# Attention and gated MLP on one core: each batch's last four output units are made among the next batch's value units, and the planner that orders the program gets other dependencies and costs

## The chip, the core and the metric

The kernel runs on one core of one Trainium2 chip. The metric is the device time of one execution in microseconds (us). The core's engines are named as in its profile: PE (matmul; PEld is its weight load, which runs beside it), DVE, ACT and POOL (elementwise work), and SP, which here only issues DMA transfers.

## What is computed

Eight batches, eight heads each, 576 tokens, head width 64. Attention with a causal mask and a cumulative bias makes x; a gated MLP with a spatial gate follows:

```
scores = q @ k.T / 8 + min(bias, 0), causal          # bias from cumsum(max(s, 0))
x      = softmax(scores) @ v                         # heads side by side: 576 x 512 per batch
h      = gelu(x @ w_in)                              # 576 x 1024
u, v   = h[:, :512], h[:, 512:]
v_n    = layernorm(v) * g_ln
v_s    = w_sg @ v_n + b_sg[:, None]                  # mixes tokens
out    = x + (u * v_s) @ w_out
```

## The kernel before

float32 products are made as three matmuls of split operands (high and low parts), accumulated in PSUM; heads 0 to 11 use plain float32 in attention.

The MLP of a batch is cut into units. Each fills one of three PSUM banks (`psm`), taken in turn in the order in which the units are written down:

- `v0` to `v4`: value units, 128 tokens each (`v4`: 64), matmuls `psm<-wi,xs` of 512 columns. An elementwise chain follows: ACT square, DVE `vt<-vt,psm`, ACT tanh, DVE `psm<-vt,psm`, DVE statistics `bs`, `mv`, DVE `vt<-psm,mv,g_b`. The last of these is what frees the bank.
- `u00` to `u13`: twelve matmuls `psm<-xs,wi` of 288 columns (half of the tokens, 128 features), then the same gelu chain.
- `s00` to `s13`: spatial gate, matmuls `psm<-ws,vn` and `psm<-wr,vnr`; the result times u is split into `gt`.
- `o00` to `o13`: twelve matmuls `psm<-gt,wo`, one DVE operation `u<-psm,xr` (half the sum plus the residual), one store `out_t<-u`. The first digit is the token half, the second the group of 128 features.

Attention of a head has scores (`pss<-k,q`), a masked minimum on DVE (`p<-pss,mask`), exp on ACT, normalising on POOL (`p<-p,rs`), transposes on PE (`psp<-ident,r`), their evacuation to `pah`, `pal`, `pbh`, `pbl`, `pdh`, `pdl` by ACT and DVE, and the product `psx<-...,vs`, evacuated to `xr`. For heads from 8 on the raw keys and queries are loaded into one buffer (`raw<-in_kq`), split by ACT and POOL (`k<-raw`) and copied about by DMA (`q<-k`, `k<-k`).

Nothing is issued as it is written. The code records operations (class `Plan`): attention of head h at place h, and the MLP of batch b spread over places 8b + 9.6 to 8b + 17.6, its units in the order of the string `ORDER` (`ORD0` for the first batch, `ORDL` for the last). `Plan.add` notes which recorded operations touch the same part of a slot or PSUM bank. `Plan.order` then simulates the engines with the costs that `cost` gives, forward and backward for `ROUNDS` rounds, and fixes one order for each engine; the engines run these queues strictly in turn. The framework adds the real semaphores by its own rules, which are not those of `Plan.add`.

Of the kernel before, what the change touches and what calls it, by code (L numbers as in the profile page):

```python
# [17 lines left out]
B, H, S, D = 8, 8, 576, 64  # L18
# [19 lines left out]
ITW = [64, 192, 320, 448, 576]  # L38
PW = [64, 192, 384, 512, 576]

ORDER = ("v0 u00 v1 u01 v2 u02 v3 v4 u10 u11 s00 u12 u03 s01 s03 u13 s02 "
         "o00 o01 s10 o03 o02 s11 s12 s13 o11 o13 o10 o12")
ORD0 = ("v0 v1 v2 v3 v4 u00 u01 u02 u10 u11 s00 u12 u03 s01 s03 u13 s02 o00 o01 s10 o03 o02 s11 s12 s13 o11 o13 o10 o12")
ORDL = ("v0 u00 v1 v2 u01 u02 v3 v4 u10 u11 s00 u12 u03 s01 s03 u13 s10 "
        "s02 o00 o01 o03 o02 s11 s12 s13 o11 o13 o10 o12")
W5, W2 = 0.232, 0.133
WARM = 8
NQ = 8
# [4 lines left out]
           ws=(8.5, 11.0), wo=(10.5, 13.0), f0=9.6, x0=2.4)  # L53
LAT = dict(PE=304.0, ACT=136.0, DVE=136.0, POOL=185.0, SP=160.0)
PROBE = None
ROUNDS = 7
N3 = 12
XR = 14

# [5 lines left out]
def _cols(ap):  # L65
    n = 1
    for _, c in list(ap.ap)[1:]:
        n *= c
    return n


def _is_ap(x):
    return hasattr(x, "ap") and hasattr(x, "tensor")


class Plan:
# [27 lines left out]
    def add(self, eng, kind, fn, args, kw):  # L104
        if "out" in kw:
            outs, rest = [kw["out"]], list(args)
        else:
            outs, rest = [args[0]], list(args[1:])
        if kw.get("accum_out") is not None:
            outs.append(kw["accum_out"])  # L110
        ins = [x for x in rest + [v for k, v in kw.items() if k not in ("out", "accum_out")] if _is_ap(x)]
        if self.open is None or self.open.eng != eng:
            o = Op()
            o.raw = set()
            o.eng, o.calls, o.deps, o.pes, o.busy, o.done, o.dma, o.kind = eng, [], set(), [], 0.0, 0.0, 0.0, kind
            k = len(self.ops)
            self.ops.append(o)
            if self.open is not None:
                self.open = o
                self.open_k = k  # L120
        else:
            o, k = self.open, self.open_k
        o.calls.append((fn, args, kw))
        cost(o, eng, kind, outs, ins, kw)
        for aps, wr in ((ins, False), (outs, True)):
            for ap in aps:
                b = self.box(ap)
                if b is None:
                    continue
                acc = self.slots.setdefault(b[0], [])  # L130
                keep = []
                for x in acc:
                    hit = x[1] < b[2] and b[1] < x[2] and x[3] < b[4] and b[3] < x[4]
                    if hit and (wr or x[5]) and x[0] != k:
                        o.deps.add(x[0])
                        if not wr:
                            o.raw.add(x[0])
                    if not (wr and hit and x[0] != k and b[1] <= x[1] and x[2] <= b[2] and b[3] <= x[3] and x[4] <= b[4]):
                        keep.append(x)
                keep.append((k,) + b[1:] + (wr,))  # L140
                self.slots[b[0]] = keep

    def group(self):
# [2 lines left out]
    def order(self, lat=LAT, rounds=None):  # L146
# [11 lines left out]
        prio = list(range(len(ops)))  # L158
        rounds = ROUNDS if rounds is None else rounds
        for i in range(rounds):  # L160
# [122 lines left out]
def cost(o, eng, kind, outs, ins, kw):  # L283
    n = _cols(outs[0])
    if eng == "PE":
        w = _cols(kw["in_"] if kind == "transpose" else ins[0])
        if kind == "transpose":
            o.pes.append((85.0 * w / P, 58.0, 165.0))
        elif ins[0].dtype == F32R:
            o.pes.append((max(54.0, 0.836 * w), 0.4397 * n + 6.4, 165.0))  # L290
        else:
            x = 0.47 * n + 45 if w == D else 0.83 * n + 95
            o.pes.append((107.0, x, 0.0))
            o.pes.append((0.0, x, 90.0))
        return
    src = ins[0] if ins else None
    psum = any("ps" == a.tensor.name[:2] for a in outs + ins)
    b = extra = 0.0
    if eng == "SP":
        q = outs[0]  # L300
        size = n * list(q.ap)[0][1] * 4
        name = src.tensor.name
        o.dma = size / (454.0 if q.tensor.name.startswith("out") else 181.0 if name.startswith("in_") else 129.5)
        return
    if eng == "ACT":
        b = 50 + 0.84 * n + (0 if psum else 40)
        if kw.get("accum_out") is not None:
            b += 204
            extra = 92
        elif _is_ap(kw.get("scale")):  # L310
            b += 95
    elif eng == "DVE":
        if kind == "tensor_tensor_reduce":
            b = 55 + 1.07 * n + (68 if _is_ap(kw["scalar"]) else 0)
        elif kind == "bn_stats":
            b = 608
        elif kind == "memset":
            b = 0.8 * n
        elif kind in ("bn_aggr", "reciprocal"):
            b = 95  # L320
        elif outs[0].dtype == I32:
            b = 480
        else:
            b = 75 + 1.03 * n + (60 if _is_ap(kw.get("scalar")) else 0) + (0 if psum else 200)
    else:
        if kind == "tensor_tensor":
            b = 535 if kw["op"] == ALU.pow else max(160, 60 + 2.36 * n)
        elif kind in ("memset", "affine_select"):
            b = 100 + n
        elif n < 8:  # L330
            b = 175
        elif kw.get("op0") == ALU.max:
            b = 850
        else:
            b = 236 + 0.83 * n
    o.busy += b
    o.done = o.busy + {"ACT": 104, "DVE": 84, "POOL": 32}[eng] + extra

# [2 lines left out]
def tile_attn_gmlp(  # L341
# [98 lines left out]
    for kind in (F32, F32R):  # L440
        v = [pools["xr"]([P, S], kind, "e", XR - 1 - i) for i in range(3)]
# [58 lines left out]
    for c0, n in ((0, 512), (512, REM)):  # L500
        ps = ps_sc.tile([P, 512], F32, name="cps", tag="sc")
        jn = NT if c0 == 0 else 5
        for j in range(jn):
            k = P if j < NT else REM
            o = max(0, j * P - c0)
# [358 lines left out]
    def ffn(b):  # L864
# [147 lines left out]
                    pools["gt"].drop(gt[ch, c])  # L1012
            yield 0.0

        unit = {"v": v_unit, "u": u_unit, "s": s_unit, "o": o_unit}
        for w in (ORD0 if b == 0 else ORDL if b == B - 1 else ORDER).split():
            yield from unit[w[0]](int(w[1]), int(w[2:] or 0))


    steps = []  # L1020
# [2 lines left out]
    def place(t, f, *args):  # L1023
        steps.append((t, next(tick), f, args))

    def spread(gen, t0, t1, total):
        done = [0.0]

        def go():
            c = next(gen, None)  # L1030
            if c is not None:
                done[0] += c
                place(t0 + (t1 - t0) * min(1.0, done[0] / total), go)

        place(t0, go)
# [20 lines left out]
    for b in range(B):  # L1056
        t0 = 8 * b + POS["f0"]
        for c in range(NC):
            place(8 * b + max(2 * c + 2.6, POS["f0"] - POS["x0"] + 0.4 * c), xsplit, b, c)
        spread(ffn(b), t0, t0 + 8.0, 53.6)  # L1060
    while steps:
        steps.sort()
        _, _, f, args = steps.pop(0)
# [58 lines left out]
```

## Time and profile before

| | us |
|---|---|
| runs | 791.68, 792.68, 795.9 (median 792.68) |
| profiled execution, its own time | 793.47 |
| its span, first to last instruction | 791.7 |
| PE busy in the span | 757.9 |
| DVE, POOL, ACT busy | 607.6, 593.5, 572.4 |

The granted TensorE clock is 0.993 of full speed over the span. Busy times overlap between engines. From about 190 us on, one batch takes some 91 us and its pattern repeats: a stretch in which value and u units run beside attention, then one of s and o units beside attention.

### The profile page before, as it was taken

The page shows a single profiled execution, that of the slowest core. Times are in us where ns is not written, and L with a number is a line of the kernel's source. Part 1 is how long each engine was busy: PE and PEld are TensorE (multiplying, and loading weights), DVE is VectorE, ACT ScalarE, POOL GpSimd, SP SyncE. Part 2 cuts the span into 40 slices and gives each one's busy share as a digit, 9 for nine tenths or more (in the row PEclk, how much of TensorE's full clock was granted, in tenths as well). Part 3 has the DMA queues.
Part 4 walks back from the last instruction along what each step waited for, and adds up shares of the span by engine and source line. Part 5 has one row for each costly group of instructions (what it writes and reads, how often), then busy time and mean ns, then how long its engine had stood idle before and what let it go on. Part 6 is the DMA issues. An engine that isn't in the chain of part 4 may idle for free.

```text
span 791.7 us, 16704 instructions
## 1 busy us (share of the span) xinstructions
PE 757.9 (96%) x5161; PEld 678.4 (86%) x5161; DVE 607.6 (77%) x1819; ACT 572.4 (72%) x1632; POOL 593.5 (75%) x981
## 2 busy tenths in 40 slices
PE   4797999999999999999999999999999999999998
PEld 3454667999889998899989998899998998899898
DVE  6788889856996679956898579966899569975662
ACT  3798789856896578956798568966799468973341
POOL 6887888867789668886789578887688767894442
PEclk9998999999999999999999999999999999999999
DMA  8476644434343543543444353334535343410101
GB/s 259 136 209 164 169 114 109 118 96 128 97 131 83 132 119 91 133 116 104 117 112 116 99 151 101 102 97 116 148 88 133 111 105 104 125 37 32 43 7 60
DMA packets 69805, 89.30 MB, mean 113 GB/s; under 512 B 25954, under 2 KB 42212, under 8 KB 69716
## 3 DMA queue, kind: packets, MB, share of 16 engines
q1 hardware_dynamic: 69716, 88.23, 41.3%
q8 instruction: 41, 0.67, 0.4%
q14 instruction: 48, 0.39, 0.2%
HBM read 42.27 MB, written 9.73 MB: 66 GB/s over the span
## 4 chain that ended last, share of the span: by engine, by line
PE 71%; ACT 9%; DVE 9%; POOL 4%; DMA 3%; issue 3%; SPq 1%; ACTq 0%; DVEq 0%; POOLq 0%
PE psm L254 43%; PE pss L254 10%; PE psx L254 9%; PE psp L254 8%; ACT p L254 3%; DVE u L254 3%; DVE p L254 2%; DMA raw<-in_kq 1%; ACT xr L254 1%; POOL vn L254 1%; POOL p L254 1%; ACT pah L254 1%; DMA q<-in_kq 1%; ACT k L254 1%; POOL k L254 1%
## 5 line engine op out<-in xcount | busy, mean ns | idle before, releaser
L254 ACT ACTIVATE p<-p,mn 128x448 f32<-128x448 f32 (+2 forms) x300 | 167.7, 561 | 45.8 <-DVE mn L254 44.5
L254 POOL TENSOR_SCALAR p<-p,rs 128x128 f32<-128x128 f32 (+3 forms) x352 | 171.1, 495 | 26.6 <-DVE rs L254 11.4
L254 PE MATMUL pss<-k,q 128*128 128x288 f32 (+9 forms) x768 | 158.7, 322 | 13.1 <-DVE mn L254 8.2
L254 PEld LDWEIGHTS pss<-k,q 128*128 128x128 f32 (+3 forms) x768 | 119.6, 184 | 40.1 <-DVE mn L254 15.9
L254 DVE CUSTOM_DVE_ANT_0 p<-pss,mask 128x448 f32<-128x448 f32 (+2 forms) x300 | 118.4, 417 | 29.2 <-PE pss L254 28.2
L254 POOL TENSOR_TENSOR k<-raw,k 128x576 fp32r<-128x576 f32 x56 | 80.0, 1429 | 60.3 <-ACT k L254 59.4
L254 PE MATMUL psm<-gt,wo 128*128 128x288 f32 x720 | 124.2, 300 | 0.0
L254 PE MATMUL psm<-xs,wi 128*128 128x288 f32 x708 | 118.5, 304 | 0.8 <-DVE vt L254 0.6
L254 PE MATMUL psm<-ws,vn 128*128 128x288 f32 x708 | 116.3, 298 | 0.0
L254 PE MATMUL psm<-wi,xs 128*128 128x512 f32 (+1 forms) x392 | 110.7, 406 | 0.3 <-DVE vt L254 0.3
L254 PEld LDWEIGHTS psm<-gt,wo 128*128 128x128 f32 x720 | 105.4, 188 | 2.0
L254 PEld LDWEIGHTS psm<-xs,wi 128*128 128x128 f32 x708 | 99.4, 188 | 4.2 <-DVE u L254 1.5
L254 PEld LDWEIGHTS psm<-ws,vn 128*128 128x128 f32 x708 | 101.4, 188 | 0.6
L254 PE MATMUL psp<-ident,r 128*128 128x128 f32 x780 | 93.7, 241 | 7.9 <-POOL p L254 6.8
L254 PEld LDWEIGHTS psp<-ident,r 128*128 128x128 f32 x780 | 83.8, 138 | 20.1 <-POOL p L254 12.1
L254 POOL TENSOR_TENSOR gt<-u,gt 128x288 fp32r<-128x288 f32 (+1 forms) x66 | 53.0, 809 | 35.5 <-ACT gt L254 32.3
L254 PEld LDWEIGHTS psm<-wi,xs 128*128 128x128 f32 (+1 forms) x392 | 68.6, 184 | 12.7 <-DVE vt L254 0.4
L254 ACT CAST pbh<-psp 128x512 fp32r<-128x512 f32 x104 | 49.7, 478 | 25.2 <-DVE u L254 15.9
L254 DVE TENSOR_TENSOR pbl<-psp,pbh 128x512 fp32r<-128x512 f32 x104 | 57.2, 550 | 5.3 <-ACT pbh L254 4.8
L254 DVE SCALAR_TENSOR_TENSOR u<-u,psm 128x288 f32<-128x288 f32 x118 | 52.3, 444 | 9.6 <-ACT u L254 9.0
L254 ACT CAST gt<-u 128x288 fp32r<-128x288 f32 (+1 forms) x66 | 27.9, 431 | 42.3 <-DVE u L254 38.3
L254 PE MATMUL psx<-pbh,vs 128*128 128x320 f32 (+3 forms) x152 | 58.3, 414 | 0.1
(140 smaller groups left out, 1627.6 us busy)
## 6 DMA issues: line engine op xcount, KB each, us to landing
q<-k SPq DMA_DIRECT2D x168, 144.0 KB
raw<-in_kq SPq DMA_DIRECT2D x56, 288.0 KB
vr<-in_vp SPq DMA_DIRECT2D x52, 192.0 KB
out_t<-u SPq DMA_DIRECT2D x64, 144.0 KB
k<-k SPq DMA_DIRECT2D x56, 144.0 KB
gt<-in_w_in SPq DMA_DIRECT2D x16, 256.0 KB
k<-in_kq SPq DMA_DIRECT2D x8, 288.0 KB
q<-in_kq SPq DMA_DIRECT2D x8, 288.0 KB
```

Of the source, the lines that this page charges most:

```text
L254: fn(*args, **kw)
```

## The change

The string that orders the units names the four units `o11 o13 o10 o12` of the batch before (marked `-`) between `v0` and `v4`; the first batch leaves them out, the last makes its own four at its end. A batch's units are kept so that the next batch can make them. Three edits touch only the planner: two accesses to one slot now also depend on each other where the tensor names differ, or for a PSUM bank where PE writes and another engine reads, whatever parts they touch; the masked minimum costs 68 instead of 55 ns ahead of its elements; an operation that writes 64 partitions from partition 64 on costs 220 ns more. The rounds go from seven to eight. No instruction is added or taken away.

```diff
-ORDER = ("v0 u00 v1 u01 v2 u02 v3 v4 u10 u11 s00 u12 u03 s01 s03 u13 s02 "
-         "o00 o01 s10 o03 o02 s11 s12 s13 o11 o13 o10 o12")
...
+ORDER = ("v0 o11- v1 o13- u00 v2 o10- u01 v3 o12- u02 v4 u10 u11 s00 u12 u03 s01 s03 u13 s02 "
+         "o00 o01 s10 o03 o02 s11 s12 s13")
...
+ORDL = ORDER + " o11 o13 o10 o12"
...
-ROUNDS = 7
+ROUNDS = 8
...
+                b += (ap.tensor.name if eng != "PE" or not wr else None,)
                 acc = self.slots.setdefault(b[0], [])
                 keep = []
                 for x in acc:
                     hit = x[1] < b[2] and b[1] < x[2] and x[3] < b[4] and b[3] < x[4]
+                    hit = hit or x[6] != b[5]
...
         if kind == "tensor_tensor_reduce":
-            b = 55 + 1.07 * n + (68 if _is_ap(kw["scalar"]) else 0)
+            b = 68 + 1.07 * n + (68 if _is_ap(kw["scalar"]) else 0)
...
+    if list(outs[0].ap)[0][1] == D and outs[0].offset >= D * list(outs[0].ap)[0][0]:
+        b += 220
     o.busy += b
...
-        unit = {"v": v_unit, "u": u_unit, "s": s_unit, "o": o_unit}
+        return {"v": v_unit, "u": u_unit, "s": s_unit, "o": o_unit}
+
+    units = {}
+
+    def ffns(b):
+        units[b] = ffn(b)
         for w in (ORD0 if b == 0 else ORDL if b == B - 1 else ORDER).split():
-            yield from unit[w[0]](int(w[1]), int(w[2:] or 0))
+            yield from units[b - w.count("-")][w[0]](int(w[1]), int(w[2:].strip("-") or 0))
```

The whole order of every engine is made anew by this. On PE, in the fifth batch, this is what stands behind the second value unit (bank 65) in the kernel before; `psm` is an MLP bank, `pss` scores, `psp` transposes:

```order
L254 MATMUL psm_65<-wi_113,xs_927 128x512 x3
L254 MATMUL pss_58<-k_862_931,q_864_933 128x288
L254 MATMUL pss_58<-k_863_932,q_0_39_108 128x288
L254 MATMUL pss_59<-k_862_931,q_864_933 128x288
L254 MATMUL pss_59<-k_863_932,q_0_39_108 128x288
L254 MATMUL psp_61<-ident_103,r_83 128x128
L254 MATMUL psp_61<-ident_103,r_85 128x128
L254 MATMUL psp_60<-ident_103,r_85 64x128
L254 MATMUL psp_60<-ident_103,r_84 128x128
L254 MATMUL psp_60<-ident_103,r_85 128x128
L254 MATMUL psm_63<-xs_900,wi_113 128x288 x3
```

And in the changed kernel, behind the second value unit of the same batch (bank 64):

```order
L255 MATMUL psm_64<-wi_113,xs_924 128x512 x3
L255 MATMUL psx_62<-pal_949,vs_923 128x512
L255 MATMUL psx_62<-pbh_956,vs_923 128x320
L255 MATMUL psx_62<-pbl_957,vs_923 128x320
L255 MATMUL psm_63<-xs_896,wi_113 128x288 x2
L255 MATMUL psm_65<-gt_918,wo_114 128x288 x3
L255 MATMUL psm_65<-gt_933,wo_114 128x288
L255 MATMUL psx_62<-pbh_956,vs_923 128x448
L255 MATMUL psx_62<-pbl_957,vs_923 128x448
L255 MATMUL psx_62<-pdh_960,vs_923 128x192
L255 MATMUL psx_62<-pdh_960,vs_923 128x64
L255 MATMUL psm_65<-gt_933,wo_114 128x288 x2
```

An output unit of the batch before (`gt,wo`) now stands between the value units, on a bank of its own, cut in pieces.

On DVE, the third value unit's chain up to its statistics (`mv`), before:

```order
L254 SCALAR_TENSOR_TENSOR vt_984<-vt_984,psm_64 128x512
L254 ISA p_74,mn_980<-pss_58,mask_104 128x448
L254 ISA mn_980 128x1
L254 TENSOR_TENSOR xr_945<-psp_61,xr_945 64x64
L254 SCALAR_TENSOR_TENSOR psm_64<-vt_984,psm_64 128x512
L254 ISA p_73,mn_980<-pss_59,mask_36_105 128x320
L254 ISA mn_980 128x1
L254 BN_STATS bs_985<-psm_64 128x6
L254 ISA p_71,mn_980<-pss_58,mask_104 64x64
L254 ISA mn_980 64x1
L254 TENSOR_TENSOR pal_979<-psp_60,pah_978 128x512
L254 BN_AGGR mv_986<-bs_985 128x2
```

Five more attention operations (three masked minima with their reads, an `xr` and a `pbl`) stand behind this before the operation that frees the bank, ten in all since the chain's first operation. The same unit in the changed kernel, from the chain's second DVE operation to the one that frees the bank:

```order
L255 SCALAR_TENSOR_TENSOR psm_64<-vt_985,psm_64 128x512
L255 BN_STATS bs_986<-psm_64 128x6
L255 ISA p_69,mn_998<-pss_58,mask_104 128x448
L255 ISA mn_998 128x1
L255 ISA p_66,mn_998<-pss_58,mask_104 64x64
L255 ISA mn_998 64x1
L255 BN_AGGR mv_987<-bs_986 128x2
L255 TENSOR_TENSOR xr_984<-psp_60,xr_984 64x64
L255 TENSOR_TENSOR xr_984<-psx_62,xr_984 64x512
L255 SCALAR_TENSOR_TENSOR vt_985<-psm_64,mv_987,g_b_107 128x512
```

Between the chain's first operation and this piece stand only a reciprocal, `pdh` and `pdl`, so seven attention operations in all stand within the chain.

On SP, between the loads of two heads' keys in the same stretch, before:

```order
L254 DMA raw_983<-in_kq 128x576
L254 DMA q_907_976<-k_906_975 64x576
L254 DMA k_905_974<-k_905_974 64x576
L254 DMA k_906_975<-cum 2x576
L254 DMA vr_968<-in_vp 128x384
L254 DMA q_929_998<-k_927_996 64x576
L254 DMA q_1_41_110<-k_927_996 64x576
L254 DMA q_929_998<-k_928_997 64x576
L254 DMA raw_1011<-in_kq 128x576
```

And in the changed kernel:

```order
L255 DMA out_t<-u_923_992 128x288
L255 DMA k_924_993<-k_924_993 64x576
L255 DMA k_925_994<-cum 2x576
L255 DMA vr_991<-in_vp 128x384
L255 DMA q_947_1016<-k_945_1014 64x576
L255 DMA q_0_39_108<-k_945_1014 64x576
L255 DMA out_t<-u_944_1013 128x288
L255 DMA q_947_1016<-k_946_1015 64x576
L255 DMA raw_1025<-in_kq 128x576
L255 DMA k_945_1014<-k_945_1014 64x576
```

Two stores of output units now stand ahead of a head's copies and key load.

## Rows read from the trace of the kernel before

**Rows 1.** The page's first part: busy time of each engine, its share of the span, and its instructions.

```profile
span 791.7 us, 16704 instructions
PE 757.9 (96%) x5161; PEld 678.4 (86%) x5161; DVE 607.6 (77%) x1819; ACT 572.4 (72%) x1632; POOL 593.5 (75%) x981
```

**Rows 2.** Four stretches of the span: length, then busy time and instructions of PE, PEld, DVE, ACT and POOL, the granted TensorE clock, the share of the DMA engines, GB/s.

```profile
0.00:80.00 80.00, 60.04 (x261) 34.56 (x261) 63.28 (x202) 56.85 (x173) 63.54 (x97) 0.96 0.66 193
80.00:140.00 60.00, 56.00 (x346) 40.34 (x347) 54.75 (x155) 52.39 (x147) 51.22 (x88) 0.96 0.49 125
140.00:690.00 550.00, 544.29 (x3866) 510.13 (x3865) 430.35 (x1320) 419.10 (x1202) 426.64 (x707) 1.00 0.43 113
690.00:791.70 101.70, 97.57 (x694) 93.42 (x692) 59.21 (x143) 44.02 (x113) 52.09 (x92) 1.00 0.13 39
```

**Rows 3.** PE's waits from 140 to 690 us: who was waited for, us in total, times, the longest.

```profile
PE psp L254 <- POOL p L254: 2.7, 6, 0.5
PE psx L254 <- ACT pah L254: 1.5, 5, 0.3
PE pss L254 <- DVE mn L254: 1.3, 5, 0.3
```

**Rows 4.** PE's longest waits from 0 to 140 us, and its only one from 690 us on.

```profile
PE pss L254 <- DVE mn L254: 6.2, 6, 1.9
PE pss L254 <- DVE vn L254: 5.3, 1, 5.3
PE pss L254 <- DMA cum<-xs: 4.9, 1, 4.9
PE psp L254 <- POOL p L254: 4.1, 4, 1.8
...
PE pss L254 <- DVE mn L254: 0.8, 1, 0.8
```

**Rows 5.** One batch in its two stretches (columns as in rows 2): value and u units, then s and o units.

```profile
464.80:516.00 51.20, 50.15 (x335) 45.12 (x334) 45.94 (x139) 44.25 (x125) 41.36 (x79) 1.00 0.46 119
516.00:556.30 40.30, 40.30 (x309) 39.56 (x309) 25.99 (x83) 25.55 (x77) 29.89 (x40) 1.00 0.39 108
```

**Rows 6.** PE in order of time in the same batch: start, duration, operation; at the end an idle time and what ended it.

```profile
473.10 3.04 PE L254 MATMUL psm<-wi,xs 128*128 128x512 f32 x12
475.98 0.70 PE L254 MATMUL pss<-k,q 128*128 128x288 f32 x4
476.51 0.52 PE L254 MATMUL psp<-ident,r 128*128 128x128 f32 x5
476.87 1.81 PE L254 MATMUL psm<-xs,wi 128*128 128x288 f32 x12
478.51 2.97 PE L254 MATMUL psm<-wi,xs 128*128 128x512 f32 x12
481.32 0.40 PE L254 MATMUL psx<-pah,vs 128*128 128x512 f32 x1
...
482.73 0.34 PE L254 MATMUL psx<-pdl,vs 128*128 128x192 f32 x1
482.90 1.26 PE L254 MATMUL pss<-k,q 128*128 128x448 f32 x8
483.99 0.41 PE L254 MATMUL psm<-wi,xs 128*128 128x512 f32 x1
...
502.68 0.33 PE L254 MATMUL psx<-pdl,vs 128*128 128x192 f32 x1
503.51 0.54 PE L254 MATMUL psp<-ident,r 128*128 128x128 f32 x4 [0.50 <-POOL p L254]
```

**Rows 7.** The engines behind that wait: POOL in order of time, and from the chain of work that ended last the load of a head's keys.

```profile
498.99 1.44 POOL L254 TENSOR_TENSOR k<-raw,k 128x576 fp32r<-128x576 f32 x1
500.41 3.04 POOL L254 TENSOR_SCALAR p<-p,rs 128x448 f32<-128x448 f32 x6
...
500.45 3.37 DMA raw<-in_kq
```

**Rows 8.** DVE in order of time: the end of the second value unit's chain and the third one's; and the evacuation to `xr` of an even head (474.01) and an odd one (488.27), each with its neighbours.

```profile
473.65 0.43 DVE L254 SCALAR_TENSOR_TENSOR u<-u,psm 128x288 f32<-128x288 f32 x1
474.01 0.68 DVE L254 TENSOR_TENSOR xr<-psx,xr 64x512 f32<-64x512 f32 x1
474.61 0.67 DVE L254 TENSOR_TENSOR pal<-psp,pah 128x512 fp32r<-128x512 f32 x1
...
480.87 0.75 DVE L254 SCALAR_TENSOR_TENSOR vt<-psm,mv,g_b 128x512 f32<-128x512 f32 x1
...
488.17 0.07 DVE L254 DVE_READ_ACCUMULATOR2_ANT mn<- 128x1 f32 x1
488.27 0.69 DVE L254 TENSOR_TENSOR xr<-psx,xr 64x512 f32<-64x512 f32 x1
488.99 0.69 DVE L254 TENSOR_TENSOR pbl<-psp,pbh 128x512 fp32r<-128x512 f32 x1
489.60 0.74 DVE L254 SCALAR_TENSOR_TENSOR vt<-psm,mv,g_b 128x512 f32<-128x512 f32 x1
```

**Rows 9.** Groups of equal instructions in one batch: count, busy us, mean ns of one, idle time before them.

```profile
L254 DVE SCALAR_TENSOR_TENSOR u<-psm,xr 128x288 f32<-128x288 f32 x8 | 3.4, 454 | 3.0 <-PE psm L254 2.8
L254 DVE SCALAR_TENSOR_TENSOR u<-u,psm 128x288 f32<-128x288 f32 x16 | 7.1, 443 | 1.2 <-ACT u L254 1.2
L254 PE MATMUL psm<-wi,xs 128*128 128x512 f32 x48 | 12.6, 401 | 0.0
L254 PEld LDWEIGHTS psm<-wi,xs 128*128 128x128 f32 x48 | 8.6, 188 | 1.6
```

**Rows 10.** All engines in order of time at the end of the span.

```profile
786.80 1.62 PE L254 MATMUL psm<-gt,wo 128*128 128x288 f32 x11
```

More of the change, by code (lines that the diff above doesn't have):

```diff
@@ L39 @@
 PW = [64, 192, 384, 512, 576]
-ORDER = ("v0 u00 v1 u01 v2 u02 v3 v4 u10 u11 s00 u12 u03 s01 s03 u13 s02 "
-         "o00 o01 s10 o03 o02 s11 s12 s13 o11 o13 o10 o12")
-ORD0 = ("v0 v1 v2 v3 v4 u00 u01 u02 u10 u11 s00 u12 u03 s01 s03 u13 s02 o00 o01 s10 o03 o02 s11 s12 s13 o11 o13 o10 o12")
-ORDL = ("v0 u00 v1 v2 u01 u02 v3 v4 u10 u11 s00 u12 u03 s01 s03 u13 s10 "
-        "s02 o00 o01 o03 o02 s11 s12 s13 o11 o13 o10 o12")
+ORDER = ("v0 o11- v1 o13- u00 v2 o10- u01 v3 o12- u02 v4 u10 u11 s00 u12 u03 s01 s03 u13 s02 "
+         "o00 o01 s10 o03 o02 s11 s12 s13")
+ORD0 = "v0 v1 v2 v3 v4 u00 u01 u02 u10 u11 s00 u12 u03 s01 s03 u13 s02 o00 o01 s10 o03 o02 s11 s12 s13"
+ORDL = ORDER + " o11 o13 o10 o12"
 W5, W2 = 0.232, 0.133
@@ L139, in add @@
                         keep.append(x)
-                keep.append((k,) + b[1:] + (wr,))
+                keep.append((k,) + b[1:5] + (wr, b[5]))
                 self.slots[b[0]] = keep
@@ L1059, in tile_attn_gmlp @@
             place(8 * b + max(2 * c + 2.6, POS["f0"] - POS["x0"] + 0.4 * c), xsplit, b, c)
-        spread(ffn(b), t0, t0 + 8.0, 53.6)
+        spread(ffns(b), t0, t0 + 8.0, 53.6)
     while steps:
```

## The prediction

> **What bounds the kernel now.** I read the page's busy times first: PE works 757.9 of 791.7 us, and the next engine, DVE, 607.6 [rows 1]. No matmul is added or taken away, so the time can change only by what PE waits, and the question is where its 33.8 idle us lie. The view by stretches puts them in three places [rows 2]: 0 to 140 us, 23.96 us (140 less 60.04 and 56.00); 140 to 690 us, only 5.71; the rest, 4.13, most of it behind the last matmul. In the middle the waits are few and of three kinds, 16 in all: transposes for POOL's normalised rows, products for ACT's copy, scores for DVE's minimum [rows 3].
>
> Then I cut one batch at its first s unit. In the stretch of value and u units PE idles 1.05 us of 51.20 and DVE, ACT and POOL are busy 90, 86 and 81%; in that of s and o units PE never idles and they are at 64, 63 and 74% [rows 5]. The elementwise work is bunched under the first. One wait shows it: POOL finishes a key split of 1.44 us at 500.43 and only then normalises, until 503.45; the transposes start at 503.51 [rows 6, 7].
>
> **What an idle us is worth.** After the product matmul at 482.73 the next starts 0.17 us later. After the one at 502.68 it is 0.83, so 0.66 is lost where the view shows 0.50 idle [rows 6]: a wait also costs 0.16 of overlap between matmuls. The 16 waits then cost 5.71 + 16 x 0.16 = 8.3 us, which is all there is to win from 140 to 690 us.
>
> **The moved units.** In the order of PE, a batch's first stretch held 56 value, 8 output, 96 u and 171 attention matmuls; now it is 56, 48, 84 and 168 or 180. So 40 output matmuls come in and 12 of a u unit go out. A matmul of 288 columns takes 0.137 us (twelve from 476.87 to 478.51 [rows 6]): 5.5 us in, 1.6 out, PE's stretch grows by 3.8 us to 55.0, and the other shrinks by as much; on PE the move costs nothing. DVE gets some three operations `u<-psm,xr` of 0.454 us and loses two u operations of 0.443 [rows 9]: 45.94 + 1.4 - 0.9 = 46.4 us, and its share falls from 90 to 84% (46.4 of 55.0). POOL and ACT get nothing, and go from 81 to 75 and from 86 to 80% even before the u unit's share leaves ACT. If instead attention follows the longer stretch at the rate of the other one, 26 us of DVE per 40.3, DVE gets up to 2.5 us more and stands at 89%: no relief at all. The counted attention matmuls hardly grow, so I take a value nearer to the first: two thirds of the 8.3 us go, **-5.5 us**; the ends are 0 and -8.3.
>
> **The planner's own edits** cost no time on the chip; they decide how well the order fits it. The 220 ns can be tested. The even head's evacuation at 474.01 starts 0.07 us before its forerunner ends and is overlapped 0.08 by its follower; the odd head's, which writes the upper partitions, starts 0.03 after and is followed 0.03 after [rows 8]: 0.10 + 0.11 = 0.21 us lost at equal durations. The new cost is about right, and the old order was made without it. The dependencies cannot be tested so, but they can only move planned times toward what the semaphores enforce. The rounds are worth nothing that a row shows.
>
> **The opening.** Of its 23.96 idle us, 5.3 and 4.9 are the first cumulative sums and their way through memory [rows 4], ahead of all that the order can change. The other 13.8 us go with minima (6.2) and POOL (4.1) that come late, while the weights are prepared. All of this is ordered anew: the first value matmuls stand about two heads earlier on PE. What that gives no row can say. The clock is at stake too: granted is 0.96 in both opening stretches, where PE waits, and 1.00 afterwards [rows 2], so a little of PE's work there ran at 1.2 instead of 2.4 GHz. I bound it by 8 us either way, a little over half of the 13.8, and take **-3**, because a planner with truer costs errs less.
>
> **What could be late next.** A value unit holds its PSUM bank until DVE has run its last chain operation. The second to fourth value units now share one bank (the order shows 64 twice). The third one's matmuls run in the old kernel from 478.51 to 481.48 and the bank is free at 490.34, after 8.9 us; the second's from 473.10 to 476.14, free at 481.62, after 5.5 [rows 6, 8]. In the new order PE has between third and fourth unit: 15 output matmuls (2.0 us), 12 of u (1.6), a head's ten products (1.6, from 481.32 to 482.90), ten score matmuls (1.09 for eight, 0.27 for two of 288), eleven transposes (0.8, five take 0.36) [rows 6]: 7.4 us. Ten attention operations stood in DVE's chain where the bank was held 8.9 us, six where it was 5.5, seven now: I take 6.3, so the bank is free 1.1 us early and costs nothing. At 8.9 it would cost 1.5 us twice a batch, 18 us over six batches, more than the gain: the cover is thin, but it exists.
>
> The stores move with their units: SP issues the same number, but two now stand between key loads that had none, and behind each stand copies `q<-k` and the next head's key load.
>
> **The end.** The last batch runs beside almost no attention, PE waits there once for 0.8 us [rows 4], and 3.3 us follow its last matmul (786.80 + 1.62 to 791.7 [rows 1, 10]). Its own output units stay last; nothing changes.
>
> **Sum.** The profiled execution took 793.5, its span and 1.8 around it, 0.8 above the median. 793.5 - 5.5 - 3 = 785.0, or 784.2 beside the median; I say **784.5 us**.
>
> **Rivals.** *Nothing changes* (0.22): POOL's bursts make the waits, and they are as long wherever output units stand; the waits of 0.3 to 0.5 us that repeat each batch speak for it, POOL's 81% against. 791 to 793 us.
>
> *The opening gives much more* (0.12): 8 us or more of the 13.8, with the middle's 5.5 and the clock: 779 or less. For it speaks that all engines wait there in turn, against it that the three elementwise engines are already busy for 79, 71 and 79% of the first 80 us [rows 2].
>
> *Slower, by the store queue* (0.12): SP takes its transfers in turn. A store waits for its output unit's DVE operation, which waits for twelve matmuls cut in pieces; a key load behind it takes 3.37 us, stood on the chain at 500.45 [rows 7] and feeds copies and the next scores. If stores hold loads back so that PE waits over 2.0 us more per batch, six batches eat the gain and 796.6 is passed; at 3 us it is 784.5 + 18 = 802. Against it: the transfers keep the DMA engines only 46% busy there [rows 5], and key loads wait for their single buffer anyway. The counterpart is an opening that loses its 8 us, which gives 795.
>
> *Far more room* is what a rule suggests. PE's weight loads fill 45.12 of 51.20 us in the first stretch and 39.56 of 40.30 in the second [rows 5]; at the second's share the first would last 45.95 us, six batches 31 us less, 761 us. But value matmuls stream 512 columns, 12.6 us busy over loads of 8.6 [rows 9], which explains 4.0 of the 6.1 us without a load, and the idle time 1.05: this room is not waiting, and the chance is 0.02, inside that of the opening. The rule is in the Trainium skill, "Perfetto Trace Analysis", Identifying the Most-Contended Engine: to judge TensorE by weight-load share, not by matmul busy time. Here the idle view carries the forecast.
>
> **Numbers.** The forecast, 780 to 788.5, has 0.54. Half a per cent (4 us) is about what a measurement of this kernel tells from no change. Faster, under 788.7: 0.54 + 0.12, less a little for the forecast's own upper edge, 0.65; same 0.23; slower 0.12. From 776 to 795 all but some 0.05 below and 0.1 above is held.
>
> **What would show it.** Right: from 140 to 690 us PE idles 2 to 3 us instead of 5.7, DVE is near 84% in the first stretch and its share rises in the second; value units start without a wait for `vt`. Wrong: waits of PE for scores behind late key loads, with stores just ahead on SP; waits of value matmuls for DVE; an opening whose idle time has grown beyond 24 us.

## The result, and the profile after

The changed kernel takes 781.62 us (780.09 to 782.38), the kernel before on the same chip 792.98 (791.68 to 795.9): a ratio of 0.9849, 95% interval 0.9818 to 0.9881, so faster by 11.4 us or 1.5%. The forecast was 784.5, from 776 to 795, and faster. Two of its three steps do not stand as written, though: the largest term was too small by half, and the reason for the second is wrong.

The first part of the page, and four stretches of the span of the changed kernel (columns as in [rows 2]):

```profile
span 778.3 us, 16742 instructions
...
PE 750.4 (96%) x5161; PEld 679.1 (87%) x5161; DVE 610.3 (78%) x1819; ACT 571.8 (73%) x1632; POOL 595.4 (76%) x981
...
0.00:80.00 80.00, 61.82 (x275) 37.36 (x276) 67.58 (x205) 58.16 (x177) 62.45 (x97) 0.94 0.65 194
80.00:140.00 60.00, 55.45 (x354) 42.33 (x352) 53.06 (x156) 52.78 (x150) 53.87 (x89) 0.97 0.54 134
140.00:690.00 550.00, 548.21 (x3938) 517.82 (x3936) 444.22 (x1365) 430.75 (x1239) 438.71 (x727) 1.00 0.43 114
690.00:778.30 88.30, 84.94 (x601) 81.61 (x600) 45.44 (x95) 30.07 (x70) 40.34 (x69) 1.00 0.10 32
```

PE idles 22.73 us up to 140 (23.96 before), 1.79 from 140 to 690 (5.71 before) and 3.36 behind that (4.13). That is only 5.9 us of the 13.4 by which the span is shorter. PE's own busy time, with the same 5161 matmuls, has fallen from 757.9 to 750.4 [rows 1]. The busy time must have held waiting. (The 38 more instructions than before are waits on semaphores; each engine's own count is the same.)

PE's waits from 140 to 690 us in the changed kernel, then its longest up to 140:

```profile
PE pss L255 <- DVE mn L255: 1.0, 2, 0.5
PE psm L255 <- DVE vnr L255: 0.3, 1, 0.3
PE psm L255 <- DVE u L255: 0.2, 1, 0.2
...
PE pss L255 <- DVE mn L255: 5.6, 7, 1.9
PE pss L255 <- DVE vn L255: 5.3, 1, 5.3
PE pss L255 <- DMA k<-xs: 4.5, 1, 4.5
PE psp L255 <- POOL p L255: 3.3, 3, 2.7
```

The waits for POOL's rows and ACT's copies that [rows 3] show in the middle are gone. No wait for a DMA stands there.

**Where waiting hides in busy time.** The kernel before, PE in order of time, behind the wait shown in [rows 6]:

```profile
503.51 0.54 PE L254 MATMUL psp<-ident,r 128*128 128x128 f32 x4 [0.50 <-POOL p L254]
503.88 0.50 PE L254 MATMUL pss<-k,q 128*128 128x288 f32 x2
504.41 0.53 PE L254 MATMUL psm<-xs,wi 128*128 128x288 f32 x2
504.77 0.45 PE L254 MATMUL psp<-ident,r 128*128 128x128 f32 x4
```

From the two score matmuls to the next row are 0.53 us; in [rows 6] the same distance holds four of them (475.98 to 476.51). So 0.26 us are lost, and the rows leave only 0.03 us of idle time there (503.88 + 0.50 to 504.41): in these rows a group of matmuls reaches beyond the start of the next (476.51 + 0.52 us against 476.87), and the part of a delay that is shorter than that overlap stands inside the busy time. So I measured waiting in another way for all that follows. The **lost time** of a matmul is the distance from its start to the start of the next, less the median of that distance for matmuls of the same operands and size in the kernel before (0.133 us for 288 columns of an MLP unit, 0.234 for 512). Its sum is 76.4 us before and 62.9 after. Both kernels run the same 5161 matmuls, so the difference, 13.5 us, has to be that of the spans, 13.4; what the measure adds is the place. Its level hangs on which matmuls are taken as the same (for the middle before, 23 to 30 us); the difference of the two middles hardly does (10 to 11 us). It splits so:

```
lost time, us                                     before   after
start to the second batch's first value matmul      49.7    46.9
from there to the eighth batch's (six periods)      26.9    16.0
the rest                                            -0.2     0.0
```

Not all of it is waiting. At some changes from one kind of matmul to another 0.04 to 0.11 us are lost, at 223 of 1245 changes before and 239 of 1320 after, 17.0 and 17.9 us in the six periods, and 16.0 to 19.2 in all the other kernels. Most of them are the first matmul of another kind behind transposes: 152 of the 164 such matmuls before lose 0.055 to 0.1 us, and 169 of 171 after. So this part differs by some 3 us at most, where the middles differ by 19.

Delays over 0.12 us make 10.9 of the 26.9 us, about four a batch, and 3.3 of the 16.0. In the middle batches before they are the same four each time: 0.65 us ahead of transposes that wait for POOL's rows, 0.2 of the 0.26 at the row of 503.88, 0.4 ahead of scores that wait for DVE's minimum, and 0.46 ahead of products that wait for ACT's copy. The changed kernel has one of 0.69 us, ahead of scores that wait for DVE's minimum, in every second middle batch.

The six periods, not the opening, hold most of the gain. A period of four middle batches is 91.4 us before and 89.35 after on average. Cut at the first s unit, as in [rows 5], the fifth batch of the changed kernel is:

```profile
452.20:505.00 52.80, 52.27 (x358) 47.96 (x358) 45.97 (x140) 44.23 (x125) 41.01 (x76) 1.00 0.45 119
505.00:541.00 36.00, 36.00 (x278) 35.28 (x278) 25.49 (x80) 25.46 (x74) 30.16 (x44) 1.00 0.41 114
```

Of the lost time of a batch, 3.75 us lay in the first of these stretches before and 0.79 in the second; now they are 1.66 (a mean over four batches, 1.17 and 2.1 to 2.2 in turn; the batch shown is one of the better two) and 0.85.

### The profile page after: what moved, and what is told of

It reads as the page before. It is cut to its first block, busy times and chain, and to the rows that moved or that the text cites. A ratio compares the mean times of both kernels' runs of the same rounds, so it can differ in the third digit from the quotient of the medians.

```text
span 778.3 us, 16742 instructions
## 1 busy us (share of the span) xinstructions
PE 750.4 (96%) x5161; PEld 679.1 (87%) x5161; DVE 610.3 (78%) x1819; ACT 571.8 (73%) x1632; POOL 595.4 (76%) x981
## 4 chain that ended last, share of the span: by engine, by line
PE 76%; DVE 6%; POOL 6%; ACT 5%; DMA 4%; issue 2%; SPq 1%; POOLq 0%; ACTq 0%; DVEq 0%
PE psm L255 45%; PE pss L255 12%; PE psx L255 10%; PE psp L255 8%; DVE u L255 2%; POOL p L255 2%; ACT p L255 2%; DMA q<-k 1%; POOL k L255 1%; DVE p L255 1%; POOL rt L255 1%; POOL u L255 1%; DMA gt<-in_w_in 1%; DMA raw<-in_kq 1%; DMA k<-xs 1%
## 5 line engine op out<-in xcount | busy, mean ns | idle before, releaser
L255 POOL TENSOR_SCALAR p<-p,rs 128x320 f32<-128x320 f32 (+3 forms) x352 | 171.2, 493 | 29.2 <-DVE rs L255 12.0
L255 ACT ACTIVATE p<-p,mn 128x448 f32<-128x448 f32 (+1 forms) x300 | 167.7, 561 | 26.2 <-DVE mn L255 24.8
L255 DVE CUSTOM_DVE_ANT_0 p<-pss,mask 128x448 f32<-128x448 f32 (+1 forms) x300 | 119.8, 419 | 22.5 <-PE pss L255 19.0
L255 PE MATMUL psm<-xs,wi 128*128 128x288 f32 x720 | 123.1, 302 | 0.4 <-DVE u L255 0.2
L255 PE MATMUL psm<-ws,vn 128*128 128x288 f32 x708 | 120.1, 300 | 0.3 <-DVE vnr L255 0.3
L255 PEld LDWEIGHTS psm<-xs,wi 128*128 128x128 f32 x720 | 103.0, 188 | 2.7 <-DVE u L255 1.1
L255 PEld LDWEIGHTS psp<-ident,r 128*128 128x128 f32 x780 | 86.1, 138 | 13.6 <-POOL p L255 4.3
L255 POOL TENSOR_TENSOR gt<-u,gt 128x288 fp32r<-128x288 f32 (+1 forms) x66 | 53.1, 809 | 42.1 <-ACT gt L255 42.1
L255 ACT ACTIVATION_READ_ACCUMULATOR p<-p,mn 128x1 f32 (+1 forms) x300 | 57.4, 191 | 0.0
L255 PE MATMUL psx<-pbh,vs 128*128 128x320 f32 (+3 forms) x152 | 56.5, 405 | 0.4 <-ACT pbh L255 0.4
```

Of the source, the lines that this page charges most:

```text
L255: fn(*args, **kw)
```

## The experiments

All were compared with the kernel before on the same chip. "Lost, middle" is the sum over the six periods, "lost, opening" that up to the second batch's first value matmul, each in the one profiled execution, which can lie some us off the median. The kernel without gelu leaves out the gelu of the u half. Every row is planned anew. The rows come together here, sorted by the number of output units carried into the next batch; each experiment follows below.

```
kernel                           units  rounds  time us  ratio   95% interval     period  lost middle  lost opening
planner's edits, old order         0      8     800.21  1.0091  1.0071 to 1.0111   92.3      31.7         51.9
before                             0      7     792.98                             91.4      26.9         49.7
before, 8 rounds                   0      8     794.17  1.0017  1.0000 to 1.0034   90.8      23.8         49.8
two units among the value units    2      8     792.29  0.9997  0.9985 to 1.0009   91.0      23.8         52.9
two units behind them              2      8     790.70  0.9972  0.9959 to 0.9984   90.3      20.4         53.4
after, no dependency edit          4      8     792.65  1.0003  0.9984 to 1.0021   90.4      20.7         57.4
four between the next u units      4      8     788.22  0.9934  0.9916 to 0.9953   89.9      20.1         54.3
after, no 220 ns                   4      8     784.36  0.9902  0.9889 to 0.9915   89.8      18.9         48.4
units moved, old planner           4      7     784.09  0.9891  0.9878 to 0.9905   89.7      18.2         48.7
after, 7 rounds                    4      7     787.79  0.9922  0.9899 to 0.9945   89.8      17.1         48.7
after                              4      8     781.62  0.9849  0.9818 to 0.9881   89.4      16.0         46.9
four behind the value units        4      8     777.55  0.9814  0.9796 to 0.9832   89.0      13.1         45.9
the same, 11 rounds                4     11     781.83  0.9865  0.9844 to 0.9886   89.1      12.9         51.5
before, a u unit without gelu      0      7     785.68  0.9900  0.9884 to 0.9916   90.2      19.1         48.6
```

**The change in its two halves.** First the units moved alone, with the old planner; then the planner's edits and 8 rounds with the old order:

```
-ROUNDS = 8
+ROUNDS = 7
...
-                b += (ap.tensor.name if eng != "PE" or not wr else None,)
...
-                    hit = hit or x[6] != b[5]
...
-            b = 68 + 1.07 * n + ...
+            b = 55 + 1.07 * n + ...
...
-        b += 220
```

> The output units moved, the planner as it was before (old dependencies, old costs, seven rounds). If the gain is the relief of the value and u stretch: 783 to 786 us beside 793, PE idle from 140 to 690 us down to 2 to 3 us from 5.7. If the planner's edits made it: 790 to 794 us and the idle time stays above 5.

```
-ORDER = "v0 o11- v1 o13- u00 v2 o10- u01 v3 o12- u02 v4 u10 ... s13"
+ORDER = "v0 u00 v1 u01 v2 u02 v3 v4 u10 ... s13 o11 o13 o10 o12"
```

The strings of the first and the last batch go back with it.

> The planner's edits and eight rounds, the units in the old order. If the moved units made the gain: 788 to 792 us, the opening shorter by about 3, the waits of the middle (5.7 us of idle) still there. If the planner's edits made it: 781 to 784 us, with the middle's waits gone though no output unit stands among the value units.

Measured: 784.09 us for the moved units, 8.3 less than the kernel before of the same runs (792.38); 800.21 for the planner's edits, 7.8 more. The first is as said for a gain by the moved units, and PE idles 1.13 us from 140 to 690 us, less than the 2 to 3 expected. The second lies outside both expected ranges: with the old order the edits bring more waits of PE, not fewer. From 140 to 690 us:

```profile
PE pss L256 <- DVE mn L256: 3.0, 10, 0.4
PE psp L256 <- DVE pbl L256: 1.0, 4, 0.3
PE psm L256 <- DVE u L256: 1.0, 5, 0.2
...
140.00:690.00 550.00, 543.77 (x3836) 506.65 (x3835) 425.55 (x1305) 417.92 (x1189) 424.21 (x699) 1.00 0.42 112
```

PE idles 6.23 us there, and its opening loses 51.9 us instead of 49.7. So the gain comes with the moved units, 8.3 of the 11.4 us without any edit of the planner. What the edits do depends on the order that they meet.

**How far apart are two plans of one kernel?** The same two kernels, each with the other's number of rounds (`ROUNDS = 7`, `ROUNDS = 8`).

> The changed kernel with seven planning rounds in place of eight. If units or planner edits made the gain by their mechanism: within 2 us of the changed kernel's 781.6. If every new plan simply falls some us higher or lower by luck: off by 4 us or more.

> The kernel before with eight planning rounds in place of seven. By mechanism: within 2 us of 793. By luck of the plan: off by 4 us or more, in either direction.

Measured: 787.79 us (782.9 to 789.03) and 794.17 (790.44 to 797.67). One number in the planner moves the changed kernel by 6.2 us, which was to speak for luck, and the old one by 1.8, which was not; and both of these plans scatter more from run to run than the two originals; their profiled executions (782.9 and 790.5) lie at the lower end. The six runs of the first go with their granted clock, a mean over the whole span: 0.991 at 782.9 us, 0.989 at 784.77, 0.974 at 789.03. Any edit of the planner is to be held against this.

**Two units; four in another place; the edits one by one.** Two units among the value units, `o11 o13` left at the end of their batch (the strings of the first and last batch to match); then all four in a block behind the last value unit; then the changed kernel without its dependency lines, and without its 220 ns:

```
+ORDER = "v0 o10- v1 u00 v2 o12- u01 v3 u02 v4 u10 ... s13 o11 o13"
...
+ORDER = "v0 u00 v1 u01 v2 u02 v3 v4 o11- o13- o10- o12- u10 ... s13"
```

> The changed kernel with only two of the four output units (o10 and o12) recorded between the next batch's value units; o11 and o13 stay at the end of their own batch. Theory A (each output unit between two value units gives TensorE work while the value unit's bank is read out, and shortens the waits there): moving four gave 8.3 us of 792.4, so two give about half, with the planner's edits 786 to 790, and a batch period about midway between 90.8 and 89.4 us, so about 90.1. Theory B (the gain is a matter of which plan the planner happens to find, not of the number of units moved): any value between 781 and 800, as likely at the 800.2 that these planner edits gave with the old order as at 781.6. Theory C (one unit is enough, because a single wait per batch was the matter): 781 to 783 and a period of 89.4.

> The changed kernel with the same four output units carried into the next batch, but recorded behind its last value unit instead of between the value units. Theory A (it is their place between value units, where TensorE waited for a bank, that gives the time): nothing of the gain is left, as the value units stand as dense as before; 791 to 801, period 90.8 to 92.3 us. Rival D (it is enough that the end of a batch is relieved of these units, or that the next batch's value units start earlier): 781 to 785, period 89.3 to 89.8.

Measured: 792.29, no gain, and 777.55, the best of all. The first is outside the ranges of theories A and C and leaves B, the plan found; the second is better than rival D had it, too. Theory A falls on it: nothing of the recorded order puts an output unit between value units there, and the gain is larger. The trace of that kernel has its waits in the middle reduced to two:

```profile
140.00:690.00 550.00, 548.27 (x3949) 518.46 (x3948) 446.82 (x1360) 432.89 (x1236) 438.24 (x728) 1.00 0.43 115
...
PE pss L254 <- DMA k<-k: 0.9, 1, 0.9
PE psm L254 <- DVE u L254: 0.8, 1, 0.8
```

On PE its value units now overlap the end of the batch before in another way: 23 matmuls of that batch's s units stand among the value matmuls, and none of an output unit. Cut into pieces of 10 us from a batch's first value matmul on, the lost time shows where waiting was: before, 3.34 of 4.54 us a batch lie 30 to 60 us behind it, where PE has u units and attention and then the first s units; after 1.25 of 2.50, in this kernel 0.93 of 2.16, with two units 2.74 of 4.15. The value units themselves, where I had looked for the waits of a bank, lose 0.5 to 0.6 us from the first to the last of them in the kernel before and in the best one, and 0.8 in the changed one.

> The changed kernel without the dependency edit in the planner (a tile's name taken along in the table of slots); 220 ns, 68 ns and 8 rounds kept. If the edits of the planner only draw another plan of the same worth, it lies with the others that have the moved units, 781 to 788. If the dependency edit is what the moved units need in order to be planned right, it is slower than the changed kernel's 781.6 by more than 4 us, 786 or above, with new waits of TensorE in the middle stretch. My prediction priced this edit at nothing: 782 +- 2.

> The changed kernel without the 220 ns that the planner adds to an operation that writes the upper partitions; dependencies, 68 ns and 8 rounds kept. If a truer cost of these writes shortens the opening, as my prediction's term of -3 us for the opening had it, the first batch's stretch up to 140 us is 2 to 3 us longer than in the changed kernel and the time is 784 to 785. If the edits only draw another plan, 781 to 788 with no rule as to the stretch.

Measured: 792.65 and 784.36. The first kernel meets its second condition, above 786, but less than a third of it lies where that condition put it: its middle loses 20.7 us, 4.7 more than the changed kernel (PE idles 3.68 us from 140 to 690), and its opening 57.4, 10.5 more. The second is 2.7 us slower than the changed kernel; the time is as its first condition said, but the opening is only 1.5 us longer and the middle loses 2.9 more. These 2.7 us are inside what one round more or less does. Beside the kernel with all edits undone (784.09), the one without the dependency edit is 8.6 us slower, though it stands nearer to the changed kernel. The edits do not add up; each draws another plan.

**Is it the run of u units?** Two late units, four units between the next u units, and the old order with less elementwise work in a u unit:

```
+ORDER = "v0 u00 v1 u01 v2 u02 v3 v4 o10- o12- u10 ... s13 o11 o13"
...
+ORDER = "v0 u00 v1 u01 v2 u02 v3 v4 o11- u10 o13- u11 o10- s00 o12- u12 u03 ... s13"
...
-            gelu2(ps[:, 0:CH], t)
+            nc.scalar.activation(out=t, in_=ps[:, 0:CH], func=AF.Copy, scale=2.0)
```

> The changed kernel with only two of the four output units carried over, as in the kernel with two units between the value units, but now recorded behind the last value unit, ahead of the run of u units. The traces so far put the lost time of a batch not into the stretch of the value units but 30 to 60 us behind the first value matmul, where TensorE has u units and attention alone (3.3 of 4.5 us per batch in the kernel before, 2.7 with two units among the value units, 1.3 in the changed kernel). Theory E (what counts is other matmul work inside that run of u units): two late units shorten it where two early ones did not; lost time there 1.0 to 2.0 us per batch, 784 to 788 us. Theory F (what counts is that four units are carried over): as with two early units, 790 to 794 us and 2.4 to 2.8 us lost there.

> The changed kernel with the four carried units recorded alternately with the u units behind the last value unit (o11, u10, o13, u11, o10, s00, o12, u12). Theory E: the run of u units has most foreign work in it that the order can give, so as good as or better than the four units recorded in a block behind the value units (777.6): 774 to 780 us, lost time at 30 to 60 us under 1.0 us per batch. If it is only a matter of the plan found, anywhere between 777 and 793.

> The kernel before, with its old order, in which a u unit's gelu (two operations on ScalarE, two on VectorE) is replaced by one copy on ScalarE; this leaves out the gelu of the u half. Theory G (the load of the elementwise engines in the run of u units makes TensorE's waits there): with three of four operations gone the 3.3 us lost per batch at 30 to 60 us fall to about 0.6, which is 2.7 us for each of seven batches: 771 to 777 us. Rival H (the waits come from the attention's own chain of minimum, exponential, normalising and transposing, whatever the u units give to the elementwise engines): less than 1 us per batch, 786 to 793 us.

Measured: 790.70, 788.22 and 785.68. Two late units lie nearer to theory F: 2.36 us lost at 30 to 60 us and a time in its range, though the middle loses 20.4 where two early ones have 23.8. Theory E is missed outright by the four units between the u units: 2.20 us lost there instead of under 1.0, and 788 us instead of 774 to 780; that it is only a matter of the plan found stays open for it. Without the gelu the loss at 30 to 60 us falls from 3.34 to 1.26, most of the way to the 0.6 of theory G; but 0.9 us of it come back in the rest of the batch (1.20 to 2.08), and the time is far from theory G and at the edge of rival H. So, in this one plan, the load of the u units makes some of the waits and not all.

That the load alone does not set them is seen in the second 30 us of a middle batch, from its first value matmul on. In order: before, after, two units among the value units, four behind them:

```profile
495.10:525.10 30.00, 28.95 (x211) 26.96 (x211) 27.43 (x83) 27.43 (x82) 27.19 (x47) 1.00 0.43 114
...
482.00:512.00 30.00, 29.46 (x213) 27.62 (x212) 27.53 (x86) 27.41 (x81) 24.27 (x45) 1.00 0.46 122
...
492.40:522.40 30.00, 29.01 (x205) 26.69 (x204) 26.31 (x76) 25.92 (x76) 22.78 (x45) 1.00 0.38 100
...
474.30:504.30 30.00, 30.00 (x226) 28.66 (x225) 27.65 (x87) 26.01 (x76) 24.02 (x42) 1.00 0.50 132
```

With two units DVE, ACT and POOL are each less busy than in the last row, and PE idles 0.99 us and runs 205 matmuls against 226. DVE is as busy in the fastest kernel as in the kernel before. The busy share of these engines does not tell which operation comes late.

**Place or luck?** The best kernel once more, with `ROUNDS = 11`:

> The kernel with the four units recorded in a block behind the last value unit (777.6 us), planned with 11 rounds in place of 8: another plan of the same recorded order. Theory I (the carried units and the block behind the value units make the middle of the program short, and a plan only scatters around it, most of it in the opening): between the first value matmul of the second and of the eighth batch about 13 us are lost, as with 8 rounds, where the changed kernel loses 16 and the others with four units up to 21; batch periods 88.5 to 89.3 us; 774 to 782 us in all, depending on the opening. Theory J (777.6 was a lucky plan): 16 to 20 us lost there as in the other kernels with four units, 781 to 788 us.

Measured: 781.83 us, and theory I holds in both parts: 12.9 us lost in the middle against 13.1, and the 4.3 us come from the opening, which loses 51.5 instead of 45.9. The first two stretches of the kernel with 8 rounds, then of that with 11:

```profile
0.00:80.00 80.00, 64.70 (x293) 38.22 (x293) 70.78 (x210) 60.63 (x184) 67.21 (x100) 0.91 0.68 200
80.00:140.00 60.00, 55.15 (x356) 41.46 (x356) 54.42 (x163) 52.87 (x152) 51.91 (x91) 1.00 0.49 123
...
0.00:80.00 80.00, 60.62 (x269) 36.64 (x270) 70.42 (x204) 59.13 (x179) 62.84 (x97) 0.96 0.65 195
80.00:140.00 60.00, 54.59 (x329) 41.42 (x329) 51.98 (x148) 48.33 (x138) 48.51 (x85) 0.89 0.48 120
```

PE idles 20.15 us in the one and 24.79 in the other.

**What the runs show together.** The lost time of the middle goes with the number of carried units: 23.8 to 31.7 us with none, 20.4 and 23.8 with two, 12.9 to 20.7 with four, over three, two and eight plans; the ranges with none and with four do not meet, those with two touch both. The opening goes with nothing that I varied: 45.9 to 57.4 us with four units, 49.7 to 53.4 with fewer. Together the two make up the difference of the profiled spans, as they must; the medians, which are measured apart from them, follow within 3 us: against the kernel before, the planner's edits alone have 4.8 + 2.2 = 7.0 us more lost and took 7.8 more; the kernel without the dependency edit -6.2 + 7.7 = 1.5, and took 0.1 more; the best -13.8 - 3.8 = -17.6, and took 15.0 less.

Open: why one place of the same four units loses 13 us and another 20, and which operation's lateness sets the rest. Two plans of the best order agree on 13; the place of the change was planned five times (16.0 to 20.7), each other place once.

## Why the prediction was right, and where not

**Where the waits lie: right.** The stretch of value and u units held 3.75 of a batch's 4.54 lost us, and the gain came there; the stretch of s and o units lost 0.79 and loses 0.85.

**What the middle is worth: the term that was mis-sized.** I took 8.3 us for all there is to win from 140 to 690, from idle times and 16 waits, and two thirds of it, 5.5. In the six periods (541 us) 10.9 us were won. The step that failed is the bound: "16 waits cost idle + 0.16" counts only waits that show as idle time. From 140 to 690 us there are 23 delays over 0.12 us, together about 9.4 us and not 8.3; the six periods reach to 731.9 us in the kernel before and hold three more, the 0.8 us wait of [rows 4] among them, 10.9 us in all. Of these 7.6 went, 70%: the two thirds were right. The other 3.3 us came from smaller differences. About 2 of them are delays of 0.04 to 0.11 us between matmuls of one kind, 30 before and 6 after; what makes the rest is not shown.

PE's weight-load share moved where its busy share could not: from 45.12 of 51.20 us, 88%, to 47.96 of 52.80, 91%, in the first stretch, while the lost time halved. Part of that rise is the added work alone: by estimate, (45.12 + 3.8) of (51.20 + 3.8) is 89%. This is the rule that I gave a chance of 0.02. The Trainium skill, "Perfetto Trace Analysis", Identifying the Most-Contended Engine, says that matmul busy time is not a good measure of how near a kernel is to its limit, because pipelined matmuls look smaller in the trace, and names weight-load share to use instead. The trace agrees with it in kind, as busy time fell by 7.5 us at equal work, and not in size: 27 us were lost, 17 of them at changes of kind, much the same in every kernel, and the rule's room was 31.

**The moved units: counts right, effect on the engines too large.** 48 output and 84 u matmuls stand in the stretch, as read from the order. I had it grow by 3.8 us to 55.0; it is 52.7 to 53.4, in the mean 53.1. The 3.8 us of matmuls came in, and 2.1 us of lost time went out, which I had not taken off: 51.1 + 3.8 - 2.1 = 52.8. The other stretch was to be 36.5 and is 36.0 to 36.5; DVE's share of it rose as said, from 64 to 71%. DVE's share was to fall from 90 to 84%, with 89% as "no relief at all"; it is 45.97 of 52.80, 87%. POOL has 78% (75 said), ACT 84% (80 said). The busy times themselves are nearly as I had them, in the mean of four batches 46.5 us for DVE (46.4 said), 41.4 for POOL (41.4) and 44.7 for ACT (44.25); the shares are higher because the stretch is shorter than 55.0. So the relief by share was about half of what I took it for, and yet the waits over 0.12 us more than halved. The busy share was the wrong sign to hang the relief on, as the four rows above show.

**What could be late next: right.** The value unit on the shared bank, PE and DVE of the changed kernel:

```profile
472.07 1.17 PE L255 MATMUL psm<-wi,xs 128*128 128x512 f32 x4
473.08 1.09 PE L255 MATMUL psm<-gt,wo 128*128 128x288 f32 x7
...
480.62 0.63 PE L255 MATMUL psm<-wi,xs 128*128 128x512 f32 x2
...
479.06 0.74 DVE L255 SCALAR_TENSOR_TENSOR vt<-psm,mv,g_b 128x512 f32<-128x512 f32 x1
```

The third unit's matmuls end at 473.24 and DVE frees the bank at 479.80, after 6.6 us (6.3 said); the fourth starts at 480.62, 7.5 us behind the start of the output matmuls (7.4 said). The bank is free 0.8 us early, and PE waits for none.

**The opening: the number right by luck, the reason wrong.** -3 was said, and the opening lost 2.8 us less; its idle time up to 140 us fell by 1.2 only. But "a planner with truer costs errs less" does not hold: the same edits lengthen the opening with the old order by 2.2 us, leaving the 220 ns out lengthens it by 1.5, leaving the dependencies out by 10.5, and three rounds more, in the kernel with the block, by 5.6. It is a draw with a spread of some 11 us, in which the changed kernel drew the second shortest. My bound of 8 us either way was the right thing to say, the sign was not to be had. The planner's edits, costed at nothing by themselves, belong to the same draw.

**The stores: right.** The rival *slower, by the store queue* does not appear: no wait for a DMA in PE's waits of the middle, and SP's longest there are for POOL and ACT.

**The end: right.** The one wait of 0.8 us [rows 4] is gone (it is counted in the six periods above), and 3.4 us follow the last matmul, as 3.3 did:

```profile
773.19 1.75 PE L255 MATMUL psm<-gt,wo 128*128 128x288 f32 x12
775.04 0.46 DVE L255 SCALAR_TENSOR_TENSOR u<-psm,xr 128x288 f32<-128x288 f32 x1 [1.20 <-PE psm L255]
```

The sum came out nearer than its largest term partly by luck: the profiled execution before stood 0.5 us above its median and the one after (780.09) 1.5 below, so the span fell by 13.4, the medians by 11.4, and 8.5 were forecast.

## What to carry to other kernels

Measure PE's waiting from start to start against the usual distance of the same matmul, not from idle time: where PE is over 95% busy, much of the waiting can be inside the busy time (here 4 of 10.9 us of delays over 0.12 us). Where a planner orders everything anew, make two or three plans of each version by a neutral number before a gain of one per cent is put down to an edit; split each into a steady stage, which repeats, and an opening, which is a draw. Work that can wait (here output units) is worth carrying over into the next round's dense stretch, and where it is recorded there is worth trying in more than one place.

## What the runs showed of the hardware

A wait between matmuls can leave next to no idle time in the records: 0.26 us in the rows at 503.88, with 0.03 us idle. Behind transposes the first matmul of another kind loses 0.055 to 0.1 us (152 of 164 in the middle of the kernel before, 169 of 171 in that of the changed one), and no idle time shows it. And in the opening the granted clock costs time as well as waits do, in another place in each plan. The kernel without the dependency edit, 80 to 120 us:

```profile
80.00:100.00 20.00, 15.63 (x74) 9.60 (x73) 17.75 (x38) 11.99 (x36) 14.93 (x19) 0.83 0.53 141
100.00:120.00 20.00, 17.58 (x88) 12.68 (x88) 14.25 (x50) 15.47 (x45) 15.77 (x31) 0.74 0.57 136
```

PE idles 4.37 us in the first of these 20 us, and in the second, with 2.42 idle, the granted clock is 0.74: about half of that time at 1.2 instead of 2.4 GHz. A head's eight score matmuls of 448 to 64 columns take 1.32 us in that kernel at 107.25 us, where the granted clock is 1.00, and 2.31 at 115.30, where it is 0.50. Between the two it fell, after PE had idled 1.67 us ahead of 107.04. From 140 to 690 us, where PE idles about 1% of the time or less, it is 1.00 in all of these kernels.
